# A tuned attention and mixer kernel: first batch re-ordered by engine, and one exponential map moved from block 1 into block 0

## The chip, the core and the metric

The kernel runs on one core of one Trainium2 chip. The metric is the device time of one execution in microseconds (us), as the median of several. The engines: TensorE (PE, matmuls; PEld is its weight load), VectorE (DVE), ScalarE (ACT), GpSimd (POOL) and SyncE (SP). POOL and SP here mostly start transfers.

## The reference, cut to what matters

Eight batches of linear attention (8 heads, 576 rows, head width 64), followed by a two-layer product over the rows ("token product") and one over the channels ("channel product"):

```python
phi = lambda x: np.where(x > 0, x, np.exp(x) - 1.0) + 1.0
q_p, k_p = phi(q), phi(k)
kv  = einsum('bhsd,bhse->bhde', k_p, v);  z = sum(k_p, axis=2)
x   = einsum('bhsd,bhde->bhse', q_p, kv) / (einsum('bhsd,bhd->bhs', q_p, z) + 1e-6)
# x is then (batch, 576, 512)
u   = x + (relu(x.T @ w_tok1) @ w_tok2).T      # 576 -> 256 -> 576
out = u + relu(u @ w_ch1) @ w_ch2              # 512 -> 1536 -> 512
```

## The kernel before

PE works in "blocks": block n is the channel product of batch n, a list of large pieces (twelve chunks of four 512-column matmuls each, then the second product), and between the pieces, at numbered steps, the kernel issues the work of later batches. phi is one exponential on ACT and three operations on DVE; q is then transposed by DMA. (In the first batch k's phi is not added up: its relu and its min(exp, 1) are two DVE operations, and PE sums the two.) In the profiles kv is the product of k and v, "nd" (in nd_ps) are q's products with it, numerators and denominators, "den" is the denominator alone, and the tail is the last 64 of the 576 rows (4 x 128 + 64), which are worked apart.

```python
def phi(nm, n, c):          # half c of batch n
    phi_exp(...)            # ACT:  e = exp(raw)
    phi_add(...)            # DVE:  y = raw + 1
    phi_end(...)            # DVE:  e = min(e, 1);  kp or qp = max(e, y)

def qtr_dma(n):             # two DMA transposes, SP's queue
    for a in range(2):
        nc.sync.dma_start_transpose(out=qT[n % 2][...], in_=qp[half[a]]...)

# the first batch has an order of its own (cut)
    nc.gpsimd.memset(qT[0], 0.0)          # a fill of 2368 columns on POOL ...
    for c in range(2):
        load_v0(c)                        # ... and then, on POOL too, v is asked for
...
    warm(27)                              # useless matmuls: 0.43 us apart at first, 0.22 from 4.2 us
...
    ksum_first(0, act); e_first("k", 1); warm(2)
    kv_first(0, act)                      # k'v of half 0, copied by ACT
    k_first(1, 0); qtr_first(1); k_first(1, 1)    # DVE: relu and min of k's half 1
    nd_first(0); den_first(0)
...
    mm2_first(1, [0, 1]); utr_first([0, 1], act); mm2_first(1, [2, 3])
    mm3(0, 0, range(0, 2)); utr_first([2], act); utr_first([3], dve)

# block 1 (cut)
    big = [...] + m3(1, 3) + m3t + m4(0, [4, 5, 6, 7, 8])
    at1 = {"kv": 11, "nd00": 13, ..., "mm1": 20, "mm2a": 21, ...}
    fill = [(s, lambda g=g: phi("q", 2, g)) for g, s in ((0, 0), (1, 2))]
    fill += [(3, lambda: qtr_dma(2)), (3, lambda: load_all(3, "qkv"))]
    fill += [(s, lambda g=g: phi("k", 2, g)) for g, s in ((0, 4), (1, 6))]
    fill += [(8, ...vcast(2, 0)), (9, ...vcast(2, 1, nc.vector.tensor_copy))]

# the end of the channel product: sums on DVE, stores on POOL's queue (SP's and ACT's at the very end)
def mm4_end(p, t):
    nc.vector.tensor_tensor(out=o, in0=ps, in1=u[b][:, r, :], op=ALU.add)
    ...
    put.dma_start(out=outv[...], in_=live["o"][half[e], 0:m])
```

## Time and profile before

| | kernel before |
|---|---|
| median of the three runs shown with it | 268.45 us (267.95 to 268.59) |
| span of the profiled run | 266.5 us |
| busy: PE, DVE, ACT, POOL | 96%, 59%, 50%, 12% |
| v's first matmul | 10.77 us |
| start of the channel matmuls that no longer break off | 23.03 us |
| end of the last matmul | 261.8 us |

A few more lines of the timeline are needed later. Their columns are start, length, engine, source line, operation, output<-input, shapes and count, and in brackets the idle time before it and what ended that.

```profile
10.67 0.76 DVE L331 TENSOR_SCALAR kr<-k_raw 128x1152 bf16<-128x1152 f32 x1
12.84 0.18 DVE L394 TENSOR_SCALAR den<-bank 128x20 f32<-128x20 f32 x1 [0.83 <-PE bank L378]
23.03 2.32 PE L475 MATMUL c_ps<-uT,wc 128*128 128x512 bf16 x10
...
67.11 0.77 PE L169 MATMUL kv_ps<-vs,kp 64*64 64x65 bf16 x72 [0.51 <-ACT vs L151]
...
110.73 3.96 SPq L199 DMA_TRANSPOSE qT<-qp  x2
113.48 1.22 POOL L523 DMA_DIRECT2D out_dram<-o_sb  x2 [19.96 <-DVE o_sb L518]
119.92 0.22 PE L210 MATMUL nd_ps<-kvbd,qT 128*128 128x130 bf16 x1
120.41 0.35 PE L210 MATMUL nd_ps<-kvbd,qT 128*128 128x130 bf16 x3 [0.26 <-DMA qT<-qp]
```

DVE starts the relu of k's second half at 10.67, before v has landed, so that the first denominator follows 2.07 us after v (12.84 - 10.77).

### The profile page before, as it was taken

How to read it: one execution, taken by the hardware profiler on the slowest of the kernel's cores; microseconds unless marked ns; L12 is line 12 of the kernel's file. 1: busy time of each engine (PE TensorE's matmuls, PEld its weight loads, DVE VectorE, ACT ScalarE, POOL GpSimd, SP SyncE). 2: the span in 40 equal slices, each digit the busy share in tenths (PEclk: the TensorE clock that was granted, in tenths of full speed). 3: DMA queues.
4: the chain of work that ended last, by engine and by line, in shares of the span. 5: the costliest groups of instructions: out<-in, count | busy, mean ns of one | idle time of the engine just before them, and what ended most of it. 6: DMA issues, size and time to landing. Idle time of an engine off the chain costs nothing.

```text
span 266.5 us, 5141 instructions
## 1 busy us (share of the span) xinstructions
PE 256.1 (96%) x2107; PEld 133.9 (50%) x2107; DVE 157.4 (59%) x309; ACT 132.9 (50%) x202; POOL 32.6 (12%) x54
## 2 busy tenths in 40 slices
PE   7899989999999999999999999999999999999992
PEld 3684445553744454445564554445564554444641
DVE  5864967469587876947684296938684272420121
ACT  5735764269718368525771358425870353036300
POOL 9710200110000300030001300030001300000000
PEclk9999999999999999999999999999999999999999
DMA  7999999353957695799999990671066500730043
GB/s 259 248 203 282 367 197 398 138 132 97 345 200 156 151 387 204 87 210 373 323 410 225 287 391 9 143 164 41 2 130 120 118 2 0 157 99 2 0 118 79
DMA packets 49927, 48.34 MB, mean 181 GB/s; under 512 B 30256, under 2 KB 35248, under 8 KB 49904
## 3 DMA queue, kind: packets, MB, share of 16 engines
q1 hardware_dynamic: 41824, 35.53, 45.1%
q0 software_dynamic: 7440, 11.44, 20.3%
q10 hardware_dynamic: 640, 1.05, 1.2%
q8 instruction: 16, 0.26, 0.4%
q14 instruction: 7, 0.06, 0.1%
HBM read 35.85 MB, written 9.44 MB: 170 GB/s over the span
## 4 chain that ended last, share of the span: by engine, by line
PE 78%; DVE 7%; DMA 5%; ACT 4%; issue 2%; POOL 1%; ACTq 0%; POOLq 0%
PE h_ps L501 31%; PE c_ps L475 23%; PE a_ps L248 6%; PE h_ps L261 5%; PE c_ps L489 4%; PE nd_ps L210 3%; DMA qT<-qp 3%; DMA cr<-in_v_dram 3%; DVE y L131 2%; PE kv_ps L169 1%; ACT cr L482 1%; ACT e L125 1%; DVE e L139 1%; DVE kp L140 1%; PE bank L363 1%
## 5 line engine op out<-in xcount | busy, mean ns | idle before, releaser
L475 PE MATMUL c_ps<-uT,wc 128*128 128x512 bf16 x384 | 91.3, 379 | 0.7 <-ACT uT L444 0.4
L482 ACT ACTIVATE cr<-c_ps 128x512 bf16<-128x512 f32 x93 | 54.4, 603 | 74.6 <-PE c_ps L475 74.4
L501 PE MATMUL h_ps<-wc,cr 128*128 128x512 bf16 x384 | 87.9, 379 | 0.0
L501 PEld LDWEIGHTS <-cr 128*128 128x128 bf16 x384 | 37.0, 98 | 42.1
L475 PEld LDWEIGHTS <-wc 128*128 128x128 bf16 x384 | 35.9, 98 | 37.7 <-issue 1.8
L518 DVE TENSOR_TENSOR o_sb<-h_ps,u 128x512 f32<-128x512 f32 x32 | 21.8, 688 | 27.3 <-PE h_ps L501 27.2
L523 POOL DMA_DIRECT2D out_dram<-o_sb x24 | 14.4, 606 | 155.1 <-DVE o_sb L518 155.1
L222 DVE TENSOR_TENSOR x<-nd_ps,den 128x512 bf16<-128x512 f32 (+1 forms) x42 | 25.3, 602 | 1.5
L139 DVE TENSOR_SCALAR e<-e 128x1152 bf16<-128x1152 bf16 x30 | 13.9, 463 | 12.4 <-ACT e L125 12.3
L125 ACT ACTIVATE e<-k_raw 128x1152 bf16<-128x1152 f32 x16 | 18.8, 1174 | 2.3 <-DMA k_raw<-in_k_dram 2.3
L273 DVE TENSOR_TENSOR u<-h_ps,x 128x1024 bf16<-128x1024 f32 x12 | 14.3, 1219 | 8.8 <-PE h_ps L261 8.8
L125 ACT ACTIVATE e<-q_raw 128x1152 bf16<-128x1152 f32 x16 | 18.6, 1162 | 1.1 <-DMA q_raw<-in_q_dram 1.1
L219 DVE TENSOR_SCALAR den<-nd_ps 128x8 f32<-128x8 f32 (+1 forms) x42 | 6.8, 163 | 19.7 <-PE nd_ps L210 19.2
L251 ACT ACTIVATE ar<-a_ps 128x512 bf16<-128x512 f32 x14 | 7.6, 595 | 18.1 <-PE a_ps L248 18.1
L210 PEld LDWEIGHTS <-qT 128*128 128x128 bf16 x140 | 11.4, 98 | 10.0 <-DMA qT<-qp 0.6
L261 PE MATMUL h_ps<-ar,w2p 128*128 128x512 bf16 x60 | 16.0, 379 | 0.1
L210 PE MATMUL nd_ps<-kvbd,qT 128*128 128x130 bf16 x140 | 15.3, 223 | 0.3 <-DMA qT<-qp 0.3
L248 PE MATMUL a_ps<-x,w 128*128 128x512 bf16 x56 | 14.4, 379 | 0.0
L151 ACT CAST vs<-v_raw 128x1152 bf16<-128x1152 f32 x12 | 14.0, 1163 | 0.0
L528 DVE TENSOR_TENSOR o_sb<-h_ps,ut 128x512 f32<-128x512 f32 x4 | 2.8, 690 | 18.7 <-PE h_ps L501 18.7
L131 DVE TENSOR_SCALAR y<-q_raw 128x1152 bf16<-128x1152 f32 x16 | 12.4, 775 | 0.3
L140 DVE TENSOR_TENSOR qp<-e,y 128x1152 bf16<-128x1152 bf16 x16 | 12.1, 759 | 0.6
(102 smaller groups left out, 215.4 us busy)
## 6 DMA issues: line engine op xcount, KB each, us to landing
k_raw<-in_k_dram SPq DMA_DIRECT2D x16, 576.0 KB, 8.6
q_raw<-in_q_dram SPq DMA_DIRECT2D x16, 576.0 KB, 7.2
v_raw<-in_v_dram SPq DMA_DIRECT2D x14, 576.0 KB, 10.4
out_dram<-o_sb POOLq DMA_DIRECT2D x24, 256.0 KB, 3.8
wc<-in_moe_w_ch_dram POOLq DMA_DIRECT2D x8, 384.0 KB, 9.8
out_dram<-o_sb SPq DMA_DIRECT2D x10, 128.0 KB, 2.3
out_dram<-o_sb ACTq DMA_DIRECT2D x8, 128.0 KB, 2.6
out_dram<-o_sb POOLq DMA_DIRECT2D x6, 128.0 KB, 7.3
```

Of the source, the lines that this page charges most:

```text
L125: nc.scalar.activation(out=e, in_=f, func=AF.Exp)
L131: nc.vector.tensor_scalar(out=y, in0=f, scalar1=1.0, scalar2=None, op0=ALU.add)
L139: nc.vector.tensor_scalar(out=e, in0=e, scalar1=1.0, scalar2=None, op0=ALU.min)
L140: nc.vector.tensor_tensor(out=dst.transpose([0, 2, 1, 3]), in0=e.rearrange("p (i t d) -> p i t d", i=nj, t=T), in1=y.rearrange("p (i t d) ...
L210: nc.tensor.matmul(out=o[:, a], lhsT=qT[b][:, t0:t0 + 128], rhs=kvbd[b][:, c, a], start=True, stop=True)
L222: nc.vector.tensor_tensor(out=x[b][:, rs[0]:rs[0] + m, HG * D * g:HG * D * (g + 1)].rearrange("p r (h d) -> p r h d", h=HG), in0=v_[:, :, ...
L248: nc.tensor.matmul(out=ps[:, mt], lhsT=w1t[:, b, ms] if r == R else w1[:, r, ms], rhs=x[b][:, r, :], start=(r == 0), stop=(r == R))
L261: nc.tensor.matmul(out=ps[:, i], lhsT=w2v(kt, r, b), rhs=ar[b][:, kt, :], start=(kt == 0), stop=(kt == NT - 1 and not add))
L475: nc.tensor.matmul(out=ps, lhsT=wc1[:, kj, 128 * mc:128 * mc + 128], rhs=uT[b][:, :, kj], start=(kj == 0), stop=(kj == NDM - 1))
L482: nc.scalar.activation(out=cr[b][:, mc, :], in_=ps, func=AF.Relu)
L501: nc.tensor.matmul(out=ps, lhsT=crt[:, kc, :] if t == 8 else cr[b][:, kc, 128 * r:128 * r + 128], rhs=wc2[:, kc, :], start=(kc == 0), stop ...
L518: nc.vector.tensor_tensor(out=o, in0=ps, in1=u[b][:, r, :], op=ALU.add)
```

## The change

Its intent is to keep PE from waiting in the first third of the run: v is asked for sooner by a shorter fill; the first batch's small copies go to whichever engine seems free; phi of q of batch 2 moves into the idle time of ACT in block 0; and two relus of block 1 move to DVE.

```diff
 # first batch (helpers split in two, further copies to ACT: cut)
-    nc.gpsimd.memset(qT[0], 0.0)
+    nc.gpsimd.memset(qT[0][:, pad], 0.0)          # 1216 columns
+    nc.vector.memset(qT[0][:, 0:2 * TD], 0.0)
-    warm(27)
+    warm(12)
     k_first(0, 1)
+    ksum_first(0)
+    warm(12)
...
-    ksum_first(0, act)
+    kv_first(0, dve)
     e_first("k", 1)
-    warm(2)
-    kv_first(0, act)
     k_first(1, 0)
...
-    nd_first(1)
-    mm1_first(0, range(R1))
+    nd_first_den(1)
+    mm1_first(0, range(R), [0])
+    nd_first_num(1)
+    mm1_first(0, [R], [0])
+    mm1_first(0, range(R1), [1])
...
-    mm2_first(1, [0, 1])
-    utr_first([0, 1], act)
+    mm2_first(1, [0, 1], True)                    # + x by an identity matmul, u copied by ACT
     mm2_first(1, [2, 3])
+    utr_first([0], act)
+    utr_first([1], dve)
 # block 0
+    fill += [(20 + g, lambda g=g: phi("q", 2, g)) for g in range(2)]
+    fill += [(22, lambda: qtr_dma(2)), (22, lambda: load_all(3, "qkv"))]
 # block 1
-    big = [...] + m3(1, 3) + m3t + m4(0, [4, 5, 6, 7, 8])
-    at1 = {"kv": 11, "nd00": 13, ..., "mm1": 20, "mm2a": 21, ...}
-    fill = [(s, lambda g=g: phi("q", 2, g)) for g, s in ((0, 0), (1, 2))]   (and its qtr_dma, load_all)
-    fill += [(s, lambda g=g: phi("k", 2, g)) for g, s in ((0, 4), (1, 6))]
+    big = [...] + [lambda mc=mc: mm3(1, mc, dve=mc in (4, 7)) for mc in range(3, NCH)] + ...
+    at1 = {"kv": 7, "nd00": 8, ..., "mm1": 15, "mm2a": 17, ...}
+    fill = [(s, lambda g=g: phi("k", 2, g)) for g, s in ((0, 0), (1, 2))]
...                                                (phi of q and k of batch 3 one or two steps earlier)
```

More of the change, by code (lines that the diff above doesn't have):

```diff
@@ L346, in qput_first, with ksum_first @@
         qtr_put(0, c, TS[h], live["qtr", c][h], put, qT[c])
-    def ksum_first(c, copy):
+    def ksum_first(c):
         ps = bank()[:, 0:2]
@@ L354, in ksum_first, with kput_first @@
                                  stop=(k_ is kp and t == T - 1))
+        live["ks"] = ps
+    def kput_first(c, copy):
         for i in range(2):
-            copy(out=kvbd[0][half[i], c, :, (i + 1) * D1 - 1], in_=ps[half[i]])
+            copy(out=kvbd[0][half[i], c, :, (i + 1) * D1 - 1], in_=live["ks"][half[i]])
     def kv_first(c, copy):
@@ L372, in q_cols, with nd_first_den @@
         return qT[c][:, t0:t0 + 128]
-    def nd_first(c):
+    def nd_first_den(c):
         dn = bank()[:, 0:4 * R1].rearrange("p (r i a) -> p r i a", r=R1, i=2)
@@ L379, in nd_first, with nd_first_num @@
                                  rhs=kvbd[0][:, c, a, D::D1], start=True, stop=True)
+        live["dn", c] = dn, work.tile([128, R1, HG], FP32, name="den0", tag="den0")
+    def nd_first_num(c):
         full = sm_tile().rearrange("p b (r h d) -> p (b r) h d", r=2, h=HG)
@@ L388, in nd_first @@
                     start=True, stop=True)
-        den = work.tile([128, R1, HG], FP32, name="den0", tag="den0")
-        live["nd0", c] = dn, den, full, last
+        live["nd0", c] = full, last
     def den_first(c):
-        dn, den, _, _ = live["nd0", c]
+        dn, den = live["dn", c]
         nc.vector.tensor_scalar(out=den, in0=dn.rearrange("p r i a -> p r (i a)"),
@@ L398, in num_first @@
     def num_first(c, r0, m):
-        _, den, full, last = live["nd0", c]
+        den = live["dn", c][1]
+        full, last = live["nd0", c]
         nc.vector.tensor_tensor(
@@ L403, in num_first, with mm1_first @@
             in1=den[:, r0:r0 + m, :, None].to_broadcast([128, m, HG, D]), op=ALU.mult)
-    def mm1_first(c, rs):
-        if rs[0] == 0:
+    def mm1_first(c, rs, mts=range(NT)):
+        if rs[0] == 0 and mts[0] == 0:
             live["mm1", c] = sm_tile()[:, :, 0:DM // 2] if c else bank().rearrange(
@@ L409, in mm1_first @@
         ps = live["mm1", c]
-        for mt in range(NT):
+        for mt in mts:
             ms = slice(128 * mt, 128 * mt + 128)
@@ L414, in mm1_first, with mm2_first @@
                                  rhs=x[0][:, r, COLS[c]], start=(r == 0), stop=(r == R))
-        if rs[-1] == R:
+        if rs[-1] == R and mts[-1] == NT - 1:
             nc.scalar.activation(out=ar[0][:, :, COLS[c]], in_=ps, func=AF.Relu)
-    def mm2_first(c, rs):
+    def mm2_first(c, rs, add=False):
         cs = COLS[c]
@@ L421, in mm2_first @@
         for i, r in enumerate(rs):
+            if add:
+                nc.tensor.matmul(out=ps[:, i], lhsT=identity, rhs=x[0][:, r, cs],
+                                 start=True, stop=False)
             for kt in range(NT):
@@ L424, in mm2_first @@
                     nc.tensor.matmul(out=ps[half[e], i], lhsT=w2r[:, kt, :, 2 * r + e],
-                                     rhs=ar[0][:, kt, cs], start=(kt == 0), stop=(kt == NT - 1))
-        nc.vector.tensor_tensor(out=u[0][:, rs[0]:rs[0] + 2, cs], in0=ps,
-                                in1=x[0][:, rs[0]:rs[0] + 2, cs], op=ALU.add)
+                                     rhs=ar[0][:, kt, cs], start=(kt == 0 and not add),
+                                     stop=(kt == NT - 1))
+        if add:
+            nc.scalar.copy(out=u[0][:, rs[0]:rs[0] + 2, cs], in_=ps)
+        else:
+            nc.vector.tensor_tensor(out=u[0][:, rs[0]:rs[0] + 2, cs], in0=ps,
+                                    in1=x[0][:, rs[0]:rs[0] + 2, cs], op=ALU.add)
     def mm2_first_tail():
@@ L563 @@
     nc.gpsimd.memset(w1t, 0.0)
-    nc.gpsimd.memset(qT[0], 0.0)
+    pad = slice(2 * TD, (4 * T + 1) * D)
+    nc.gpsimd.memset(qT[0][:, pad], 0.0)
+    nc.vector.memset(qT[0][:, 0:2 * TD], 0.0)
     nc.vector.memset(qT[1], 0.0)
@@ L594 @@
     k_first(0, 0)
-    warm(27)
+    warm(12)
     k_first(0, 1)
+    ksum_first(0)
+    warm(12)
     e_first("q", 0)
+    kput_first(0, act)
     q_first(0, 0)
@@ L602 @@
     q_first(1, 0)
-    qput_first(0, 0, dve)
+    qput_first(0, 0, act)
+    qput_first(0, 1, act)
     q_first(1, 1)
-    qput_first(0, 1, act)
-    ksum_first(0, act)
+    kv_first(0, dve)
     e_first("k", 1)
-    warm(2)
-    kv_first(0, act)
     k_first(1, 0)
@@ L612 @@
     k_first(1, 1)
-    nd_first(0)
+    nd_first_den(0)
+    nd_first_num(0)
     den_first(0)
@@ L616 @@
     qput_first(1, 1, act)
-    ksum_first(1, act)
+    ksum_first(1)
+    kput_first(1, act)
     kv_first(1, act)
@@ L712 @@
     utr_tail(0)
-    big = [lambda mc=mc: mm3(1, mc, range(2, 4)) for mc in range(3)] + m3(1, 3) + m3t + m4(0, [4, 5, 6, 7, 8])
-    at1 = {"kv": 11, "nd00": 13, "nd01": 14, "nd10": 15, "nd11": 16, "nd20": 17, "nd21": 18,
-           "mm1": 20, "mm2a": 21, "mm2b": 22, "mm2t": 24, "uta": 21, "utb": 22}
-    fill = [(s, lambda g=g: phi("q", 2, g)) for g, s in ((0, 0), (1, 2))]
-    fill += [(3, lambda: qtr_dma(2)), (3, lambda: load_all(3, "qkv"))]
-    fill += [(s, lambda g=g: phi("k", 2, g)) for g, s in ((0, 4), (1, 6))]
-    fill += [(8, lambda: vcast(2, 0)), (9, lambda: vcast(2, 1, nc.vector.tensor_copy))]
+    big = [lambda mc=mc: mm3(1, mc, range(2, 4)) for mc in range(3)] + [lambda mc=mc: mm3(1, mc, dve=mc in (4, 7)) for mc in range(3, NCH)] + m3t + m4(0, [4, 5, 6, 7, 8])
+    at1 = {"kv": 7, "nd00": 8, "nd01": 9, "nd10": 10, "nd11": 11, "nd20": 12, "nd21": 13,
+           "mm1": 15, "mm2a": 17, "mm2b": 18, "mm2t": 20, "uta": 17, "utb": 18}
+    fill = [(s, lambda g=g: phi("k", 2, g)) for g, s in ((0, 0), (1, 2))]
+    fill += [(4, lambda: vcast(2, 0)), (5, lambda: vcast(2, 1, nc.vector.tensor_copy))]
     fill += [(at1[nm], fn) for nm, fn in steps(2)]
-    fill += [(s, lambda g=g: phi("q", 3, g)) for g, s in ((0, 19), (1, 23))]
-    fill += [(24, lambda: qtr_dma(3)), (24, lambda: load_all(4, "qkv"))]
-    fill += [(s, lambda g=g: prep_k(3, g)) for g, s in ((0, 25), (1, 27))]
+    fill += [(s, lambda g=g: phi("q", 3, g)) for g, s in ((0, 19), (1, 21))]
+    fill += [(22, lambda: qtr_dma(3)), (22, lambda: load_all(4, "qkv"))]
+    fill += [(s, lambda g=g: prep_k(3, g)) for g, s in ((0, 24), (1, 26))]
     run(big, sorted(fill, key=lambda e: e[0]))
```

## The prediction

Cut from the text below, with the cuts marked, are general statements on the hardware that no trace of this case shows. No term of the sum is cut: it is still -0.5 + 1.2 + 0 - 0.35 = +0.35 us, hence 268.8, shaded to 268.6. The +1.2 is about what lies between 47.72, when PE took x before, and the 48.85 worked out for x's new end (1.13 us). The "two over 1152 bf16 columns" are DVE's maximum of two inputs (L140, 0.76 us) and its minimum with a constant (L139, 0.46 us), as in the timeline that the prediction quotes.

> **What bounds the kernel now.** I read the page first: busy shares, then the 40 slices of 6.66 us.
>
> ```profile
> PE 256.1 (96%) x2107; PEld 133.9 (50%) x2107; DVE 157.4 (59%) x309; ACT 132.9 (50%) x202; POOL 32.6 (12%) x54
> ...
> PE   7899989999999999999999999999999999999992
> DVE  5864967469587876947684296938684272420121
> ACT  5735764269718368525771358425870353036300
> ```
>
> TensorE (PE) bounds the run: outside the first third its slices are all 9. It is idle about 266.5 - 256.1 = 10.4 us, of which 1.4 us lie before its first matmul and 266.5 - 261.8 = 4.7 us after its last. Everything a better schedule can win is therefore (a) the remaining 4.3 us of idle time, all before about 121 us, (b) places where PE counts as busy but its matmuls stretch, and (c) useless matmuls of the first batch's warm-up. No part of the change touches the 140 us after that. A gain of 2% would be 5.4 us, more than (a).
>
> Next I cut the run by stage in windows of 2 us. The columns are length, then busy us of PE, weight loads, VectorE (DVE), ScalarE (ACT), GpSimd, then granted clock, DMA share and GB/s.
>
> ```profile
> 58.00:60.00 2.00, 2.00 (x11) 0.90 (x10) 0.97 (x2) 2.00 (x4) 0.00 (x0) 1.00 0.91 203
> 60.00:62.00 2.00, 2.00 (x11) 0.82 (x9) 1.93 (x4) 2.00 (x4) 0.00 (x0) 1.00 0.19 53
> 62.00:64.00 2.00, 1.86 (x10) 0.75 (x9) 1.93 (x4) 2.00 (x4) 0.00 (x0) 1.00 0.12 29
> 64.00:66.00 2.00, 1.86 (x9) 0.76 (x8) 1.93 (x4) 2.00 (x4) 0.00 (x0) 1.00 0.77 186
> ```
>
> From 57 to 68 us ACT is full: batch 1's first channel product waits for PSUM banks that ACT empties (relus), while the same ACT does the exponentials of batch 2's q and k. The PE timeline puts a number on it: 48 matmuls of 512 columns, 4 of the tail transpose and batch 2's kv product run from 55.11 to 67.88, 12.77 us. At 0.216 us each (a run of 4 takes 0.86 in the chain) they need 10.37 + 0.24 + 0.71 = 11.32. This stage loses **1.45 us**. It is what moving phi of q aims at.
>
> For the other parts I read the timeline of single instructions (start, length, engine, line, what).
>
> ```profile
> 1.71 2.07 POOL L564 MEMSET qT<- 128x2368 bf16 x1
> 3.73 1.66 POOL L117 DMA_DIRECT2D cr<-in_v_dram  x2
> 10.77 0.68 PE L363 MATMUL bank<-cr,kr 64*128 64x128 bf16 x18 [0.67 <-DMA cr<-in_v_dram]
> 13.44 1.56 DVE L400 TENSOR_TENSOR x<-bank,den 128x1024 bf16<-128x1024 f32 x2
> ...
> 46.60 0.42 DVE L222 TENSOR_TENSOR x<-nd_ps,den 128x256 bf16<-128x256 f32 x1
> 46.85 1.03 PE L248 MATMUL a_ps<-x,w 128*128 128x512 bf16 x4
> 47.72 0.38 PE L248 MATMUL a_ps<-x,w1t 128*128 128x512 bf16 x1
> 50.29 1.29 DVE L518 TENSOR_TENSOR o_sb<-h_ps,u 128x512 f32<-128x512 f32 x2 [3.27 <-PE h_ps L501]
> ...
> 84.67 0.75 DVE L131 TENSOR_SCALAR y<-q_raw 128x1152 bf16<-128x1152 f32 x1
> 85.33 0.45 DVE L139 TENSOR_SCALAR e<-e 128x1152 bf16<-128x1152 bf16 x1
> 85.82 0.76 DVE L140 TENSOR_TENSOR qp<-e,y 128x1152 bf16<-128x1152 bf16 x1
> 86.49 0.68 DVE L269 TENSOR_TENSOR ut<-h_ps,x 64x512 bf16<-64x512 f32 x1
> ```
>
> To see: v is asked for at 3.73, after a 2.07 us fill, and its first half lets PE go at 10.77. DVE has 3.27 us idle before 50.29, but directly before it the last x of batch 1 ends at 47.02 and PE reads it at 47.72. One phi costs DVE 84.67 to 86.49 = 1.82 us.
>
> [...] once v moves (after 7.4 us, none of its bytes before, in a view of queues over 3.7 to 7.4), the software queue has 34% and the loads of q and k 77% of the engines. [...] 0.76 against 0.46 us for the two over 1152 bf16 columns, and a relu from PSUM on DVE costs 0.68 against 0.60 us on ACT, so the two moved relus are not free. [...] Here the first seven warm-up matmuls are 0.43 us apart and the rest 0.22 from about 4.2 us[...].
>
> **The change part by part.** Built, the changed kernel has 4210 PE rows against 4216 (five warm-up matmuls fewer, two identity matmuls more, each with its weight load), and the same loads.
>
> *First batch.* The fill before v shrinks from 2368 to 1216 columns: 2.07 x 1216/2368 = 1.06, so v is asked for 1.0 us sooner. As it then shares with q and k for longer, I take its first half at about 10.0 instead of 10.7, the second halves of q and k 0.5 us later (8.4 and 10.1), v's second half unchanged. kv of half 0 then ends at 11.2 (11.95 before). But its copies (0.4 us) now stand on DVE before the relu and min of k's second half, 0.76 + 0.47, so the denominator starts at 12.9 and the first x at 13.4, as before. What is won comes after: the second key-sum is ready at 12.9 rather than 13.2, kv of half 1 ends 0.4 sooner, and x of half 1 starts near 16.0 (16.23). Then one of four u pieces goes to ACT, and the four transposes are copied by two engines: the run of unbroken channel matmuls, at 23.03 before, should begin near 22.55. **-0.5 us** (estimate -0.2 to -1.0). Behind it the loads of batch 1 leave some 0.5 us of room: k's second half lands at 28.2 (issued about 18.1, 10.1 to land) and DVE uses it at 29.17. A larger win would wait there.
>
> *Phi of q of batch 2 in block 0.* Its data are there: issued at 37.25, landing after 6.0 and 6.8 us, near 43.3 and 44.5; ACT idles from 42.86 to 49.2. But in the built order of DVE, the first phi stands before the last den, reciprocal and x of batch 1, the second after them. x ends at 47.02 + 1.82 = 48.85. The fifth matmul of the token product needs it at 47.72[...]: **+1.2 us**. The second phi (48.9 to 50.7) fits in the 3.27 us of idle time, and the output additions lose nothing.
>
> *Block 1 with its earlier steps.* ACT loses two exponentials (2 x 1.05) and two relus (2 x 0.5). That would free the 1.45 us. But kv now stands after channel chunk 7 rather than after all twelve: with dense matmuls PE arrives at 56.65 + 3 x 0.43 + 5 x 0.86 = 62.25. On DVE, from the end of the first exponential at 58.85: min and max of k, 1.27, y 0.74, min and max 1.25, the relu of chunk 4 0.62, the cast of v 0.7: 63.6. kv waits **1.4 us**. Its end, 64.4, with the four chunks (3.45) still to come, is 67.85: the same point as 67.88 before. So -1.45 + 1.4 = **0**. The wait for ACT becomes a wait for DVE.
>
> *End of block 1.* u of batch 2 is made four steps sooner, and k of batch 3 one step sooner. kv of batch 3 ran 91.02 to 92.09, 1.07 us, instead of 0.71 for the work: **-0.35**.
>
> Sum: -0.5 + 1.2 + 0 - 0.35 = +0.35, hence 268.8 us. I go a little lower, to 268.6: both new waits come from adding lengths in a DVE queue, and a change that another engineer thought worth making is likelier to beat my sum than to fall behind it. That is a choice, not a measurement.
>
> **The rivals.** (1) *The ACT wait goes and nothing replaces it*: if casts or phi are quicker than I add up, block 1 gives 1.4 and the first batch 0.5 to 1.0, for about 266.5. For it: ACT is at 2.00 of 2.00 in the windows. Against: DVE is at 1.93 there too, and gets the relus. (2) *v's earlier request wins all of 1 us or more*: 267.8 with my other terms. Against: DMA is saturated from 2 us (400 GB/s between 3.7 and 7.4 us), and batch 1's loads leave 0.5 us. (3) *Worse*: both stalls, and the later q and k cost the first batch its gain: 269.8. For it: the second exponential of q waits for its data even now (0.81 us idle before 7.87).
>
> **Range and chances.** Rivals 1 and 3 give the edges: 266.6 to 269.8, eight in ten. Two per cent is 263.1 or 273.8, outside what the idle time holds or the stalls add: faster 0.03, within 0.96, slower 0.01.
>
> **What would show it.** Right: the first v matmul near 10.0 us; a PE wait of about 1.2 us on DVE's x inside batch 1's token product; batch 2's kv waiting over 1 us for the cast of v on DVE, with chunk matmuls dense before it; no wait at batch 3's kv. Wrong: if batch 1's token product runs in 2.16 us, or kv of batch 2 starts without a wait, my DVE sums fail and the time is nearer 267. If [...] unbroken matmuls start after 23 us, the first batch has lost rather than gained.

## More of the kernel before

The transposes of batch 4's q are issued from 110.73 and the first stores of batch 2's output from 113.48, on another queue. The products of batch 4 then run one matmul and pause: the other three start 0.49 us after the first, because the second transpose has not landed.

## The result, and the profile after

The changed kernel took **271.31 us** (four runs, 270.48 to 271.76), against 268.40 for the kernel before in the same rounds (four runs, these three and one more, 267.95 to 268.59). The ratio is 1.0107, with an interval of 1.008 to 1.0135. A ratio here is the mean time of one kernel's fast runs over that of the other's of the same rounds, so it is not quite the ratio of the medians. The change is a loss of about 1%. That is inside the 2%, but outside the predicted range of 266.6 to 269.8.

The page of the changed kernel, busy shares and slices (6.75 us each):

```profile
PE 256.0 (95%) x2085; PEld 134.2 (50%) x2104; DVE 158.7 (59%) x313; ACT 132.9 (49%) x200; POOL 32.7 (12%) x54
...
PE   7899989899999999997999999999999999999993
DVE  6674876877829875955676276957684281420121
ACT  5634877149565258623773158615871354026300
```

PE's busy time is the same, 256.0 us, and the span is 3.5 us longer: nothing was added but waiting. One 8 stands in the eighth slice, where there was a 9, and a new 7 in the nineteenth slice (121.5 to 128 us), a place that the change does not touch. The table follows PE from landmark to landmark, in the timelines of both profiles.

| stretch of PE's work | before | after | difference |
|---|---|---|---|
| v's first matmul | 10.77 | 11.59 | +0.82 |
| from there to the unbroken channel matmuls | 12.26 | 13.20 | +0.94 |
| end of batch 0's u to the matmul of batch 1's token product that needs its last x | 21.70 | 22.70 | +1.00 |
| block 1, from the tail's transposes to its last matmul | 32.58 | 32.04 | -0.54 |
| end of block 1 to the kv product of batch 4 | 28.52 | 28.20 | -0.32 |
| batch 4's wait for its transposed q (first to second nd matmul) | 0.49 | 2.09 | +1.60 |
| end of the last matmul | 261.78 | 265.30 | +3.52 |

The six parts sum to +3.50 of +3.52. The stretches between them (not listed) did not change.

**First batch**, timeline after:

```profile
2.77 1.60 POOL L117 DMA_DIRECT2D cr<-in_v_dram  x2
11.59 0.68 PE L366 MATMUL bank<-cr,kr 64*128 64x128 bf16 x18 [1.35 <-DMA cr<-in_v_dram]
12.81 0.59 DVE L370 CAST kvbd<-bank 64x128 bf16<-64x128 f32 x2 [1.92 <-PE bank L366]
13.44 1.03 DVE L331 TENSOR_SCALAR kr<-k_raw 128x1152 bf16<-128x1152 f32 x1
...
24.79 2.32 PE L488 MATMUL c_ps<-uT,wc 128*128 128x512 bf16 x10
```

v is asked for 0.96 us sooner, as the diff promises, and its first matmul starts 0.82 us later. Its data do begin to move sooner, at 6.87 us instead of 7.84 (first packet of POOL's queue in the two traces), but the first half then takes longer to land (8.8 us from issue, before 7.0). On DVE the copy of kv now stands in front of the relu of k's second half: DVE idles 1.92 us for v, and that relu starts at 13.44 where before it started at 10.67.

**Token product of batch 1**, timeline after. The three DVE lines are phi of q (its last operation), then the last denominator and x; the PE line is the matmul that needs x:

```profile
48.92 0.76 DVE L140 TENSOR_TENSOR qp<-e,y 128x1152 bf16<-128x1152 bf16 x1
49.60 0.15 DVE L219 TENSOR_SCALAR den<-nd_ps 128x4 f32<-128x4 f32 x1
50.00 0.42 DVE L222 TENSOR_TENSOR x<-nd_ps,den 128x256 bf16<-128x256 f32 x1
50.48 0.38 PE L248 MATMUL a_ps<-x,w1t 128*128 128x512 bf16 x1 [1.06 <-DVE x L222]
```

This is the wait that the prediction put at 1.2 us. It measured 1.06.

**Block 1**, windows of 2 us after (length, busy us of PE, PEld, DVE, ACT, POOL, then clock, DMA share, GB/s) and its timeline:

```profile
60.00:62.00 2.00, 2.00 (x11) 0.91 (x10) 0.25 (x1) 2.00 (x4) 0.76 (x2) 1.00 1.04 371
62.00:64.00 2.00, 2.00 (x11) 0.94 (x10) 1.93 (x4) 2.00 (x4) 0.00 (x0) 1.00 0.99 318
66.00:68.00 2.00, 1.65 (x45) 1.07 (x45) 0.90 (x2) 1.16 (x4) 0.00 (x0) 1.00 1.03 408
```

```profile
65.32 0.48 PE L169 MATMUL kv_ps<-vs,kp 64*64 64x65 bf16 x36
65.55 0.75 DVE L151 CAST vs<-v_raw 128x1152 bf16<-128x1152 f32 x1
66.35 0.48 PE L169 MATMUL kv_ps<-vs,kp 64*64 64x65 bf16 x36 [0.55 <-DVE vs L151]
```

ACT is still full, but PE issues 11 matmuls per window where it issued 10 and 9. The wait at kv has moved to DVE's cast of v, as predicted, though only in front of the second 36 matmuls: the first 36 need ACT's half of v alone.

**Batch 4**, timeline after:

```profile
112.60 4.46 SPq L199 DMA_TRANSPOSE qT<-qp  x2
115.41 1.21 POOL L536 DMA_DIRECT2D out_dram<-o_sb  x2 [20.69 <-DVE o_sb L531]
121.85 0.22 PE L210 MATMUL nd_ps<-kvbd,qT 128*128 128x130 bf16 x1
123.94 0.35 PE L210 MATMUL nd_ps<-kvbd,qT 128*128 128x130 bf16 x3 [1.86 <-DMA qT<-qp]
```

The spot at which the kernel before lost 0.26 us now costs 1.86 us of idle PE. The median time of the two transposes from issue to landing is 6.8 us, against 6.0 before. Nobody touched this code; the largest single difference lies here.

### The profile page after: what moved, and what is told of

Same layout as the page of the kernel before. It is cut to its first block, busy times and chain, and to the rows that moved or that the text cites. A ratio compares the mean times of both kernels' runs of the same rounds, so it can differ in the third digit from the quotient of the medians.

```text
span 270.0 us, 5115 instructions
## 1 busy us (share of the span) xinstructions
PE 256.0 (95%) x2085; PEld 134.2 (50%) x2104; DVE 158.7 (59%) x313; ACT 132.9 (49%) x200; POOL 32.7 (12%) x54
## 4 chain that ended last, share of the span: by engine, by line
PE 82%; DMA 7%; DVE 6%; ACT 2%; issue 1%; POOL 1%; POOLq 0%; ACTq 0%
PE h_ps L514 30%; PE c_ps L488 28%; PE a_ps L248 5%; PE h_ps L261 5%; PE c_ps L502 4%; DMA qT<-qp 3%; DMA cr<-in_v_dram 3%; PE nd_ps L210 3%; PE kv_ps L169 1%; DVE x L222 1%; PE bank L419 1%; PE bank L433 1%; ACT e L125 1%; PE bank L366 1%; DVE e L139 1%
## 5 line engine op out<-in xcount | busy, mean ns | idle before, releaser
L495 ACT ACTIVATE cr<-c_ps 128x512 bf16<-128x512 f32 x91 | 53.5, 598 | 80.9 <-PE c_ps L488 80.8
L514 PE MATMUL h_ps<-wc,cr 128*128 128x512 bf16 x376 | 86.9, 379 | 0.5
L139 DVE TENSOR_SCALAR e<-e 128x1152 bf16<-128x1152 bf16 x30 | 13.9, 464 | 13.0 <-ACT e L125 12.7
L210 PEld LDWEIGHTS <-qT 128*128 128x128 bf16 x140 | 11.4, 98 | 11.6 <-DMA qT<-qp 2.2
L140 DVE TENSOR_TENSOR qp<-e,y 128x1152 bf16<-128x1152 bf16 x16 | 12.1, 758 | 0.6
## 6 DMA issues: line engine op xcount, KB each, us to landing
out_dram<-o_sb POOLq DMA_DIRECT2D x24, 256.0 KB, 4.6
```

The source lines that it names most:

```text
L139: nc.vector.tensor_scalar(out=e, in0=e, scalar1=1.0, scalar2=None, op0=ALU.min)
L210: nc.tensor.matmul(out=o[:, a], lhsT=qT[b][:, t0:t0 + 128], rhs=kvbd[b][:, c, a], start=True, stop=True)
L495: nc.scalar.activation(out=cr[b][:, mc, :], in_=ps, func=AF.Relu)
L514: nc.tensor.matmul(out=ps, lhsT=crt[:, kc, :] if t == 8 else cr[b][:, kc, 128 * r:128 * r + 128], rhs=wc2[:, kc, :], start=(kc == 0), stop ...
```

## The experiments

Theory A (from the landmarks): the first batch loses because DVE's queue stands still for v, the token product loses because phi stands before x, and batch 4 is hit by stores that happen to run into its transposes. Rivals: B, the earlier request for v is itself the harm (it delays k and q); C, the later blocks are the whole loss and the first batch only shifts it; D, the wait at batch 4 is a fixed consequence of the new schedule. Runs of one group shared their chip and the runs of the kernel before. Every output was correct. A run counts as slow when it is over 1.5% above the fastest of the same kernel; ratios use fast runs alone.

### Group 1: which part of the change costs what

**old_front**: the changed blocks behind the first batch of before.

```diff
-    (the whole new first batch)
+    (the first batch of the kernel before; block 0 and block 1 stay changed)
```

> The changed kernel with the whole first batch of the kernel before (order, warm-up, fill, u); only the later blocks are changed. Theory (the first batch lost 1.8 us, the unbroken channel matmuls began at 24.79 instead of 23.03): they begin near 23.0 again and the time is 271.3 - 1.8 = 269.5 us, less if the wait of batch 4's products for the transposed q (1.9 us in the profile of the changed kernel) is shorter by chance. Rival (the first batch is a wash and the profile of the changed kernel was an unlucky one): 271 us.

**early_v**: the kernel before, with nothing but the short fill.

```diff
-    nc.gpsimd.memset(qT[0], 0.0)
+    nc.gpsimd.memset(qT[0][:, pad], 0.0)
+    nc.vector.memset(qT[0][:, 0:2 * TD], 0.0)
```

> The kernel before with the fill split alone, so v is asked for at 2.77 instead of 3.73 us. Theory (v sent earlier among the loads of q and k does not land earlier; in the changed kernel its first half landed at 11.55 against 10.75): first v matmul at 10.8 to 11.6 us, time 268.4 to 269.2. Rival (v lands 0.7 us sooner, as the prediction had it, and something else in the changed kernel held it up): first v matmul near 10.0 us, time 267.9 to 268.4.

**late_v**: the changed kernel with the old fill.

```diff
-    nc.gpsimd.memset(qT[0][:, pad], 0.0)
-    nc.vector.memset(qT[0][:, 0:2 * TD], 0.0)
+    nc.gpsimd.memset(qT[0], 0.0)
```

> The changed kernel with the old single fill, so v is asked for at 3.73 us again. Theory (asking sooner is what made v later): first v matmul back to 10.8 us instead of 11.59, second halves of k and q earlier too, unbroken channel matmuls near 24.0 instead of 24.79, time 270.5 us. Rival (order on VectorE alone makes the loss): same 271.3 us, unbroken matmuls still after 24.6 us.

**kr_first**: the changed kernel with DVE's relu of k's second half back in front of the copy of kv.

```diff
+    k_first(1, 0)
     kv_first(0, dve)
     e_first("k", 1)
-    k_first(1, 0)
```

> The changed kernel, but on VectorE the relu of k's second half stands before the copies of kv of half 0 rather than behind them. Theory (the copies wait for v, and the relu, the min and with them the second key sum, its kv and the first x wait behind the copies): the first denominator starts about 1.0 us sooner than 14.86, the unbroken channel matmuls near 23.9, time 270.4 us. Rival (v's landing alone sets the pace): the first denominator stays within 0.3 us of 14.86 and the time at 271.3 us.

| | median us (range), 6 runs | ratio to before [95%] | v's first matmul | v to unbroken matmuls | wait of batch 4 | end of matmuls |
|---|---|---|---|---|---|---|
| before (11 runs; profile of the first reading) | 268.33 (267.65 to 270.31) | 1 | 10.77 | 12.26 | 0.49 | 261.78 |
| old_front | 268.66 (267.90 to 268.75) | 0.9995 [0.9967, 1.0023] | 11.54 | 12.26 | 0.06 | 262.28 |
| early_v | 268.65 (268.10 to 269.13) | 1.0002 [0.9971, 1.0033] | 10.89 | 12.26 | 0.06 | 261.86 |
| late_v | 270.34 (268.95 to 272.75) | 1.0070 [1.0028, 1.0113] | 11.00 | 13.11 | 0.63 | 263.28 |
| kr_first | 270.02 (268.62 to 271.91) | 1.0052 [1.0013, 1.0091] | 10.86 | 12.44 | 0.92 | 262.65 |

The changed blocks alone cost next to nothing (old_front), so rival C falls in the form that they are the whole loss. The short fill alone neither gains nor harms (early_v), and taking it out of the changed kernel does not mend it (late_v): rival B falls, and the prediction's gain from v does not show. In early_v, v was asked for at 2.77 and its first matmul still ran at 10.89:

```profile
2.77 1.60 POOL L117 DMA_DIRECT2D cr<-in_v_dram  x2
10.89 0.68 PE L363 MATMUL bank<-cr,kr 64*128 64x128 bf16 x18
```

kr_first shows the order in DVE's queue at work:

```profile
10.53 0.75 DVE L331 TENSOR_SCALAR kr<-k_raw 128x1152 bf16<-128x1152 f32 x1
12.08 0.59 DVE L370 CAST kvbd<-bank 64x128 bf16<-64x128 f32 x2 [0.80 <-PE bank L366]
12.71 0.46 DVE L335 TENSOR_SCALAR kp<-e 128x1152 bf16<-128x1152 bf16 x1
13.20 0.18 DVE L399 TENSOR_SCALAR den<-bank 128x20 f32<-128x20 f32 x1
```

The relu runs at 10.53, while DVE would otherwise wait for v, and the denominator follows 2.34 us after v (13.20 - 10.86), where in the changed kernel it took 3.27. The stretch after v shrinks from 13.1 to 12.44 us. The time does not resolve it: kr_first's runs spread over 3.3 us, and those of late_v beside it over 3.8. That scatter was a finding of its own, since old_front and early_v spread over about 1 us.

### Group 2: the scatter, phi behind x, and a mended version

**again**: the changed kernel, unaltered.

> The changed kernel unaltered, a second look beside the others of this batch. Theory (a fixed loss of about 1.1 us against the kernel before: 0.9 in the first batch after v has landed, 1.0 of token product wait, less 0.55 in block 1 and 0.3 at batch 3's kv; the rest of the 2.9 us is v's landing, 10.8 to 11.6 us, and batch 4's wait for the transposed q, 0 to 2 us, which differ from run to run): first unbroken channel matmul 13.1 to 13.2 us after the first v matmul, time 269.4 to 272. Rival (the change itself makes the wait of batch 4 longer): that wait is above 1.5 us again and the time 271 or more.

**new_front**: the new first batch with the old blocks (the reverse of old_front).

```diff
-    (block 0 and block 1 as changed)
+    (block 0 and block 1 of the kernel before; the new first batch stays)
```

> The kernel before with the new first batch alone (order, warm-up, fill, u), later blocks as before. Theory: unbroken channel matmuls 13.1 to 13.2 us after the first v matmul instead of 12.26, everything behind it as before, time 268.4 + 0.9 = 269.3 us plus what v's landing adds. Rival (the front is harmless when the blocks are old): 12.3 us and 268.4 us.

**phi_behind**: both halves of phi issued after the last x.

```diff
-    fill += [(20 + g, lambda g=g: phi("q", 2, g)) for g in range(2)]
+    fill += [(21 + g, lambda g=g: phi("q", 2, g)) for g in range(2)]
```

> The changed kernel with the first phi of q of batch 2 put behind the last x of batch 1 on VectorE. Theory (that phi held PE's token product for 1.0 us): the product runs without a wait, and the time is 1.0 us below the changed kernel of the same batch of runs. Rival (the phi only moves the wait, to the output additions or the transposes): less than 0.4 us below it.

**mended**: the kernel before, with the changed blocks, phi behind x, and kv of batch 2 two steps later than in the change.

```diff
+    fill += [(21 + g, lambda g=g: phi("q", 2, g)) for g in range(2)]       # block 0, on the old first batch
+    at1 = {"kv": 9, "nd00": 10, ..., "mm1": 17, "mm2a": 19, ...}
```

> The kernel before, its first batch untouched, with the new later blocks mended: phi of q of batch 2 behind the last x, and kv of batch 2 after channel chunk 9 instead of 7, with what follows it moved by two steps. Theory: the wait of 1.0 us in the token product and the wait of kv for the cast of v go, while the relief of ScalarE stays: -1.45 in block 1 and -0.3 at batch 3's kv, so 268.4 - 1.7 = 266.7 us. Rival (PE gains nothing there because the waits move on to the sums behind kv): 268.0 us or more.

| | median us (range), fast runs | ratio to before [95%] | v to unbroken matmuls | wait of batch 4 | end of matmuls |
|---|---|---|---|---|---|
| before (11 runs) | 268.32 (267.72 to 269.81) | 1 | | | |
| again (5 fast runs; the sixth, 273.59, slow) | 269.81 (269.46 to 273.03) | 1.0090 [1.0036, 1.0143] | 13.12 | 0.05 | 263.35 |
| new_front | 269.85 (269.08 to 270.75) | 1.0049 [1.0017, 1.0080] | 13.13 | 1.32 | 264.21 |
| phi_behind | 269.71 (269.23 to 271.38) | 1.0049 [1.0016, 1.0082] | 13.12 | 0.06 | 263.15 |
| mended | 268.91 (268.47 to 269.52) | 1.0015 [0.9984, 1.0046] | 12.26 | 0.05 | 262.54 |

The unaltered kernel's times fall in two groups: three runs of 269.46 to 269.81 us (granted clock 0.996 to 0.998), and 272.95, 273.03 and the slow 273.59 (0.993 and 0.994). Its profile here shows no wait at batch 4 and ends 1.95 us sooner than the first profile. So the wait at batch 4 belongs to some executions and not to others, which is against rival D.

new_front has the old blocks, and its stretch after v is the long one: 13.13 us. The first batch's loss is its own.

phi_behind is a miss worth reading. Batch 1's token product does lose its wait (21.69 us from the end of batch 0's u, as before the change), but the stretch behind it, up to the tail's transposes at the head of block 1, grows from 8.68 to 9.85 us:

```profile
50.28 0.76 DVE L131 TENSOR_SCALAR y<-q_raw 128x1152 bf16<-128x1152 f32 x1
52.78 0.46 DVE L139 TENSOR_SCALAR e<-e 128x1152 bf16<-128x1152 bf16 x1 [1.74 <-ACT e L125]
53.95 1.28 DVE L531 TENSOR_TENSOR o_sb<-h_ps,u 128x512 f32<-128x512 f32 x2
```

On ACT the second exponential now stands behind the relus of the token product (it starts at 51.58; in the changed kernel both were done before them). DVE waits 1.74 us for it, with the output sums of batch 0 queued behind. Behind them on DVE stand its halves of u (55.14 and 56.34), and PE's transposes of u start as these end (55.88 and 57.07). The wait was moved, not removed. mended has the same fault on the old first batch (9.85 us too).

### Group 3: the stores, u on two engines, and a better order of phi

**stores_behind**: the changed kernel; the first pair of output stores of batch 2 waits until batch 4's transposes have landed.

```diff
-            nc.sync.dma_start_transpose(
+            live["qtd", n] = nc.sync.dma_start_transpose(
...
-                    (nc.scalar if last and e else put).dma_start(...)
+                    after((nc.scalar if last and e else put).dma_start(...),
+                          live["qtd", 4] if (p, t) == (1, 1) else None)
```

> The changed kernel with one dependency added: the first pair of output stores of batch 2 waits until batch 4's transposed q has landed. Theory (the large scatter of the changed kernel, 269.5 to 273.6, comes from these stores running into the transposes of q; PE then waits up to 2 us for q[...]): batch 4's products start without a wait, no run has a mean clock under 0.995, the scatter shrinks to about 1 us and the median to about 269.5 us. Rival (the scatter comes from the first batch, v's landing[...]): median and scatter as in the changed kernel, 271.4 us, with some runs above 272.5 us at a clock of 0.993 or 0.994.

**old_u**: kr_first, with u of the first batch back on one engine and its transposes in their old order.

```diff
+    k_first(1, 0)                       # as in kr_first
...
-    mm2_first(1, [0, 1], True)
+    mm2_first(1, [0, 1])
+    utr_first([0, 1], act)
     mm2_first(1, [2, 3])
-    utr_first([0], act)
-    utr_first([1], dve)
```

> The changed kernel with the relu of k's second half ahead of the kv copies on VectorE, as before, and in addition u and the transposes of the first batch as in the kernel before (four VectorE additions, no identity matmuls, transposes of columns 0 and 1 together). Theory (two engines for u gain nothing[...]): the unbroken channel matmuls begin 12.1 to 12.3 us after the first v matmul instead of 12.44. Rival (u on two engines is a gain that the order of VectorE covered up): 12.7 us or more. In time the two are too near for the scatter; the profile decides.

**mended2**: the first batch of before. In block 0 both exponentials are issued early; one half's DVE work comes behind x, the other half's moves to the head of block 1, where DVE idled 1.8 us. One relu of block 1 on DVE instead of two.

```diff
+    fill += [(20, lambda g=g: phi_exp("q", 2, 2 * g, 2)) for g in range(2)]
+    fill += [(21, lambda: phi_add("q", 2, 0, 2)), (21, lambda: phi_end("q", 2, 0, 2))]
 # block 1
+    big = [...] + [lambda mc=mc: mm3(1, mc, dve=mc == 7) for mc in range(3, NCH)] + ...
+    at1 = {"kv": 8, "nd00": 9, ..., "mm1": 16, "mm2a": 18, ...}
+    fill = [(0, lambda: phi_add("q", 2, 2, 2)), (0, lambda: phi_end("q", 2, 2, 2)),
+            (0, lambda: qtr_dma(2)), (0, lambda: load_all(3, "qkv"))]
```

> The old first batch; both exponentials of q of batch 2 on ScalarE before the token product's relus; the rest of its first half on VectorE behind the last x, that of its second half at the start of block 1, where VectorE is idle for 1.8 us; the relu of channel chunk 4 back on ScalarE; kv of batch 2 after chunk 8. Theory (each moved wait is met: token product, output additions, kv): -1.3 in block 1, -0.2 at batch 3's kv, nothing lost before, so 268.3 - 1.5 = 266.8 us. Rival (the transposes of q of batch 2, now asked for 6 us later, or VectorE again, hold PE): 268 us or more.

**mended2_stores**: mended2 with the dependency of stores_behind.

> The same, with the dependency of the first pair of output stores of batch 2 on batch 4's transposed q. Theory: batch 4's wait (0.05 to 2 us) is gone in every run, so 266.5 us with a scatter of under 1 us. Rival (the stores held back run into a later transfer, or the wait was not theirs): no better than the run without it.

| | median us (range), fast runs | ratio to before [95%] | v to unbroken matmuls | wait of batch 4 | end of matmuls |
|---|---|---|---|---|---|
| before (11 runs) | 268.24 (267.54 to 270.72) | 1 | | | |
| stores_behind | 269.39 (268.93 to 269.92) | 1.0030 [0.9997, 1.0063] | 13.12 | 0.06 | 263.46 |
| old_u (5 fast runs, one slow: 302.76) | 268.66 (268.26 to 268.92) | 1.0004 [0.9971, 1.0037] | not read | not read | not read |
| mended2 | 266.91 (266.27 to 267.71) | 0.9941 [0.9909, 0.9973] | 12.26 | 0.05 | 260.91 |
| mended2_stores | 266.92 (266.20 to 267.13) | 0.9938 [0.9908, 0.9968] | 12.27 | 0.05 | 260.68 |

With one dependency more the scatter is gone. The six runs of stores_behind lie within 1.0 us, against 3.6 us for the five fast runs of the same kernel without it (in group 2, on another chip), and no run had a granted clock under 0.996. The two ratios, 1.0030 and 1.0090, have intervals that overlap, and the two were not run on one chip, so the mean alone would not decide. In mended2, whose profile has no wait, the same dependency changes nothing (266.91 and 266.92 us). The timeline of stores_behind shows what the dependency does:

```profile
112.27 4.11 SPq L199 DMA_TRANSPOSE qT<-qp  x2
120.16 2.40 POOL L536 DMA_DIRECT2D out_dram<-o_sb  x4 [25.74 <-DMA qT<-qp]
121.56 0.40 PE L210 MATMUL nd_ps<-kvbd,qT 128*128 128x130 bf16 x4
```

The stores wait, the transposes land in a median of 4.9 us instead of the 6.8 of the first profile, and the four matmuls run as one group.

old_u's profile (clock 0.854) gives no landmarks; its timed fast runs are level with before. mended2 beats both kernels. In its timeline, x stands ahead of phi, the matmul that needs x comes without a wait, and the second half's DVE work lies at 57.08, in block 1:

```profile
47.25 0.42 DVE L222 TENSOR_TENSOR x<-nd_ps,den 128x256 bf16<-128x256 f32 x1
47.59 0.75 DVE L131 TENSOR_SCALAR y<-q_raw 128x1152 bf16<-128x1152 f32 x1
48.37 0.38 PE L248 MATMUL a_ps<-x,w1t 128*128 128x512 bf16 x1
57.08 0.75 DVE L131 TENSOR_SCALAR y<-q_raw 128x1152 bf16<-128x1152 f32 x1
63.99 0.78 PE L169 MATMUL kv_ps<-vs,kp 64*64 64x65 bf16 x72
```

Its kv product runs as one group of 72 without a wait, and block 1 takes 31.35 us against 32.58 before.

### Group 4: does the kernel before suffer too, and four more looks

**before_stores**: the kernel before, with only the dependency of stores_behind.

> The kernel before with the dependency alone: the first pair of output stores of batch 2 waits for batch 4's transposed q. Theory (the collision is already in the kernel before, only seldom: of its 33 runs beside the three batches, five lie at 269.8 us or more): no run above 269 us, median 268.0 us. Rival (the few slow runs before have another cause): some runs at 269.5 us or more again.

**old_u2** (old_u again), **look1** and **look2** (the changed kernel again), one look each.

> The kernel with the old u, seen again because its profile fell in the slow state. Theory: unbroken channel matmuls 12.1 to 12.3 us after the first v matmul (12.44 with u on two engines). Rival: 12.7 us or more.

> The changed kernel, for one more profile. If this is a run of the long kind (272.5 us or more): theory, a wait of 2 us or more for the transposed q of batch 4[...]. If it is of the short kind (269.5 us): no such wait[...].

> The changed kernel, for one more profile, with the same expectations as the other look.

| | median us (range) | v's first matmul | v to unbroken matmuls | wait of batch 4 | end of matmuls |
|---|---|---|---|---|---|
| before (10 fast runs, one slow: 688.54) | 268.62 (267.96 to 269.35) | | | | |
| before_stores (6 runs) | 268.09 (267.46 to 268.74), ratio 0.9983 [0.9963, 1.0002] | 10.59 | 12.27 | 0.05 | 261.16 |
| old_u2 (1 run) | 268.35 | 10.65 | 12.18 | 0.06 | 261.87 |
| look1 (1 run) | 270.98 | 10.89 | 13.12 | 2.08 | 264.52 |
| look2 (1 run) | 271.98 | 11.64 | 13.08 | 1.98 | 265.52 |

The expectation of before_stores counts five of the 33 earlier runs of the kernel before at 269.8 us or more; recounted, it is four (269.81 twice, 270.31, 270.72). With the dependency, none of six passed 268.74. That fits, but the interval still holds 1.

old_u2 gives what old_u could not: 12.18 us after v, against 12.44 in kr_first and 12.26 in the kernel before. look1 and look2 show the long wait twice more. In four profiles of the changed kernel the wait of batch 4 is 2.09, 0.05, 2.08 and 1.98 us: a collision that happens or does not.

The kept traces show what goes with it. Fourteen fast or single profiles leave the stores free. The wait follows the time from the first store's issue to its first packet:

| profiles with the stores free | store's issue to its first packet | wait of batch 4 |
|---|---|---|
| after, look1, look2 | 1.50 to 1.52 us | 1.98 to 2.09 us |
| new_front, kr_first, late_v | 1.60 to 1.71 us | 0.63 to 1.32 us |
| before | 2.09 us | 0.49 us |
| again, phi_behind, old_front, early_v, mended, mended2, old_u2 | 2.39 to 2.60 us | 0.05 or 0.06 us |

The sooner the store's data move behind the transposes, the longer PE waits.

## Why the prediction was wrong, point by point

**The first batch: predicted -0.5 us, measured about +0.9.** This is the step that failed: the prediction paid for a worse order on DVE with an earlier v, and no earlier v came. The +0.9 is the stretch behind v (13.20 or 13.12 us instead of 12.26). Three of its terms were wrong.

The first is "I take its first half at about 10.0 instead of 10.7". v's first matmul ran at 10.59 to 11.54 us in seven profiles with the old fill (middle value 11.37) and at 10.65 to 11.64 in ten with the short one (middle of the two central values 11.16). Asking 0.96 us sooner brought no gain that stands out of that scatter, and early_v, where nothing else differs, shows none in the time. The request did reach the engines sooner: the first packet of v moved at 6.83 to 6.92 us in the ten and at 7.84 to 8.16 in the seven. What was gained there went in a slower transfer beside q and k. The prediction itself had read 400 GB/s between 3.7 and 7.4 us, with none of v's bytes among them, and POOL's queue at 34% of the engines beside 77% for q and k from 7.4 to 8.4; it should have drawn the consequence. From before to after, v's request went from 7.0 to 8.8 us to landing, and k's second half from 7.3 to 9.1.

The second follows from it. The prediction saw that the kv copies now stand ahead of the relu of k's second half, and let v's early landing pay for it. Without that landing the full price appears. By kr_first, restoring the order is worth 13.12 - 12.44 = 0.68 us. The trace shows that the relu did not overtake: DVE idles 1.92 us, up to 12.81, for v's product with a relu behind it whose data came at about 11.4 (issued at 2.27, 9.1 us to land; ACT reads the same data from 11.38).

A third, smaller piece is u on two engines: 12.44 - 12.18 = 0.26 us by old_u2, where the prediction counted a gain. Read from the timelines, not taken apart by a run: in the old order eight transposes of u run ahead of the last eight token matmuls (20.04 to 20.99), which hide 0.64 of the 1.01 us of their copy to uT (PE idles 0.43 for it); in the new order all of them come behind, and PE idles 0.45 for the copy. With both orders undone the stretch is 12.18 us, level with the 12.26 before, and old_u's time is level too (1.0004).

**The token product: predicted +1.2, measured +1.00** (PE idle 1.06). The step was right in mechanism and nearly in size; the same +1.00 is in old_front and not in new_front.

**Block 1: predicted 0, measured -0.54.** Right mechanism (ACT's wait becomes a wait for DVE's cast), wrong size: the wait at kv was sized at 1.4 us and measured 0.55. The DVE sum itself came out: the second 36 matmuls start 7.19 us after the tail's transposes (66.35 - 59.16), where the prediction had 63.6 - 56.40 = 7.20. But it made all 72 wait for DVE's cast, and half of v is cast by ACT. The 26 chunk matmuls before kv were not quite dense either: 5.92 us, where 26 x 0.216 is 5.62.

**End of block 1: predicted -0.35, measured -0.32.** Right.

**What was not in the prediction: the stores.** It said that "No part of the change touches the 140 us after that", and its search for idle time ended at about 121 us. The loss of up to 1.6 us lies at 122 us. The line that would have warned was in the profile before: the split of batch 4's matmuls, one and three. That the stores cause the wait rests on four observations together, since a single profile with a short wait proves nothing (again had one too). In all three profiles with the stores held back (stores_behind, mended2_stores, before_stores) the wait is 0.05 or 0.06 us; with the stores free, the four profiles of the changed kernel have it three times at about 2 us. In those three the transposes land in a median of 6.8 us; with the stores held back in 4.5 to 4.9, and in again, where the store's data moved late, in 4.6. Over fourteen profiles the wait falls as the store's data move later (the table above). And of eleven runs of the changed kernel (four of the first reading, the five fast ones of again, look1, look2) eight were above 270 us, of the six of stores_behind, on another chip, none.

The sum of the steady parts is now +0.9 + 1.0 - 0.54 - 0.32 = +1.04 us. stores_behind, the changed kernel without the collision, measured 269.39 - 268.24 = +1.15 (by the ratio +0.8, with an interval from about 0 to +1.7). That is nearest to the prediction's third rival (both stalls, first batch loses), and its sign for it, unbroken matmuls after 23 us, came true at 24.79. The rest of the measured +2.9 us is laid to the collision (+1.60 in the first profile) and to v's chance landing (+0.82 there).

**The shading.** The working summed to 268.8 us, and was shaded to 268.6 on the ground that a change is likelier to beat a sum than to fall behind it. Here that went the wrong way. The terms that worked out adverse waits were about right; the optimistic one, v, was not.

**The warm-up.** The prediction read the warm-up matmuls 0.43 us apart at first and 0.22 from about 4.2 us, and took it that fewer of them change nothing. Over the profiles the narrower spacing came at 4.14 to 7.25 us, run by run (5.25 to 7.04 in four of the changed kernel, 4.14 to 7.19 in seven with the old first batch); the two overlap, and no difference could be laid to it. The first batch's loss appears after v (10.59 us at the earliest), with the spacing already narrow. The granted clock does not tell the two spacings apart: it reads 1.00 from 2 to 4 us (wide) and from 8 to 10 us (narrow), in the profiles before and after.

**What stays open.** First, why the changed kernel collides more often. Its stores are issued at the same distance behind the transposes (2.81 us after, 2.75 before), but the first packet follows in 1.5 to 1.7 us in some runs and in 2.1 to 2.6 in others, and no run says why. Two things go with the early packet, neither tested. SP is longer at issuing the two transposes (4.46 to 4.82 us in the six profiles with a wait over 0.5, 3.51 to 3.97 in the other eight). And all six have the new first batch or most of it (out of nine such, none out of five with the old order). Second, three long runs of the changed kernel (271.36, 272.95 and 273.03 us) had a granted clock of 0.991 to 0.994, and the wait of 2 us alone does not make 273 us. No profile caught such a run, so what made up the rest is not shown. Third, phi_behind and mended show that the moved wait costs 1.17 us, but how much of it ACT's order makes and how much the output sums' was not parted.

## What to carry to other kernels

Before moving an instruction to an "idle" engine, ask what stands behind it in that engine's queue, and keep anything that waits for a late transfer behind everything whose data are already there (here DVE idled 1.92 us before such a copy, with a relu behind it). A request made sooner on DMA engines that are already full is worth nothing until the trace shows that it landed sooner (here it was made 0.96 us sooner, and the first matmul came at 11.59 us instead of 10.77). And when two transfers on different queues come within microseconds of each other, look at that spot in several profiles: here the scatter was 3.6 us without and 1.0 us with a single dependency (on two chips), at a place that the diff does not mention.
